# Moving the V loads of an attention and FFN kernel from SyncE's queue to GpSimd's

## The chip, the cores and the metric

The kernel runs on one core of a Trainium2 chip. The metric is the device time of one execution in microseconds (us). A run is called slow when it is over 1.5% above the fastest of the same kernel. "Faster", "same" and "slower" are drawn at 2%.

## The reference

Attention is computed inside chunks of 64 tokens; its output, laid out as tokens by 512, goes through two matrices with a squared ReLU between them.

```python
batch, n_heads, seq, head_dim = (8, 8, 576, 64)          # 4608 tokens of 512
n_tokens, d_model, d_ff = (4608, 512, 2048)
...
scores = scale * np.matmul(q_c, k_c.transpose(0, 1, 2, 4, 3))   # chunks of 64
attn = softmax(scores)                                          # cut
out = np.matmul(attn, v_c)
...
h = np.maximum(x @ w_in, 0.0)
return (h * h @ w_out).astype(np.float32)
```

## The kernel before

The 4608 tokens are 18 groups of 256; two groups make a block, and there are nine blocks, 0 to 8. While TensorE does the two FFN matrix products of block j, the attention of block j+1 (`nxt`) is threaded in between, and q, k and V of block j+2 (`far`) are loaded. Nearly all loads are issued from SyncE (`nc.sync`), nearly all stores of results from ScalarE.

```python
def v_pieces(g):                      # four or five loads for one group
    for t, p, m, b, s in runs(g):
        yield lambda ...: nc.sync.dma_start(
            out=v_even[g % NV][p:p + m, t, :, 0:D],
            in_=v[b, 0::2, s:s + m, :].rearrange("h s d -> s h d"))
    ...                               # the same for the odd heads, into v_odd

def cast_qk(g):                       # GpSimd: float32 to bfloat16
    qkb = att_pool.tile([128, 2, 2 * H * D], BF16, name="qkb", bufs=2)
    for which in range(2):
        nc.gpsimd.tensor_copy(out=qkb[:, which], in_=...)

def transpose_qk_dma(g):              # one DMA transposes q and k of a group
    qkT = att_pool.tile([128, 2, 2, n_hp, 128], BF16, name="qkT", bufs=4)
    nc.sync.dma_start_transpose(out=qkT..., in_=qkb...)
```

`scores` reads qkT with 32 small matmuls, `values` reads v_even and v_odd, and `transpose_x` brings the attention output x into the layout of the FFN, from block 3 on with two more DMA transposes a group from SyncE. In the second FFN product every 16 matmuls end in a copy and a store, both on ScalarE:

```python
nc.scalar.copy(out=o_sb, in_=o_ps)
nc.scalar.dma_start(out=out[t0:t0 + 128, :], in_=o_sb)
```

A plan lays these pieces into slots; a slot is four FFN matmuls. In each slot at most one load is issued.

```python
else:                                             # blocks 2 to 8
    loads, go_slots = pieces(far), range(32)      # q and k of both groups, then V
    d = {2: 5, 3: 2}.get(j, 0)
    for i, g in enumerate(nxt):
        for slot, f in ((4, SC), (8, AV), (11, XT)):
            at(slot + d if f is SC else slot + d + 3 * i, f, g)
    for i, g in enumerate(far):
        at(14 + 2 * i, C, g)                      # casts
        at(19 + 3 * i, TD, g)                     # DMA transposes of q and k
```

The softmax here doesn't subtract the row's maximum and nothing guards it: scores larger than these inputs give would overflow.

## Time and profile before

| | before |
|---|---|
| median of 3 runs | 302.27 us (299.15 to 306.41, the last of which counts as slow) |
| profiled span | 302.7 us |
| TensorE busy | 280.5 us, 93% |
| GpSimd busy | 49.4 us, 16% |
| DMA transposes of q and k, issue to landing, median | 4.9 us |

TensorE is nearly always busy, so what counts is when it isn't. The prediction reads the page, the stretches, the waits and SyncE's queue. Two more readings matter for what follows. The first is the view of the source line of the q and k transposes (columns of its first line: duration of the issuing instruction in ns as minimum, median and maximum, then first and last start in us):

```profile
L224 SPq DMA_TRANSPOSE qkT<-qkb x14: 1655/2552/3704, 69.1 to 233.3; - x14
...
DMA to landing us min/median/max: 4.0/4.9/6.5
```

No transpose needs more than 6.5 us. The second is the DMA view from 69 to 76 us, while the first pair of them is under way (a queue's packets, MB, and the time of its packets as a share of the 16 engines' time, which can pass 100%):

```profile
q1 hardware_dynamic: 5224, 1.31, 105.5%
```

All that moves here goes through one queue, q1: 1.31 MB at 209 GB/s, and the pair, issued from 69.10 on, has landed at 76.21.

### The profile page before, as it was taken

To read this page: it belongs to the slowest core of one execution; us is meant where nothing else is said; L and a number is where in the kernel's file an instruction comes from. 1 tells how busy PE (TensorE), PEld (TensorE's weight loads), DVE (VectorE), ACT (ScalarE), POOL (GpSimd) and SP (SyncE) were. 2 spreads that over 40 slices of the span, in tenths; PEclk is the share of its full clock that TensorE was granted. 3 is DMA by queue.
4 is the path that set the end of the run, shared out by engine and by line. 5 is a ranking of instruction groups with operands and counts; after the bars stand their busy time and mean duration, and the time that the engine had idled before them with its cause. 6 is when DMAs were issued, how large, how long until landed. Compare 5 with 4: busy or idle time off the path is not lost.

```text
span 302.7 us, 6379 instructions
## 1 busy us (share of the span) xinstructions
PE 280.5 (93%) x2564; PEld 141.3 (47%) x2598; DVE 113.0 (37%) x247; ACT 130.0 (43%) x225; POOL 49.4 (16%) x68
## 2 busy tenths in 40 slices
PE   2889979898899799899999997999999999999995
PEld 2654435784454444444444443444444444444442
DVE  1348613692234350353037203740482038104400
ACT  1536305674217621762176215731662186217511
POOL 2047820140130040023003201400230000000000
PEclk9999999999799999999999999999999999999999
DMA  7999999999999899999899899869997704211011
GB/s 207 243 347 365 342 264 246 237 206 212 217 213 211 194 191 205 224 215 193 195 250 211 148 229 269 171 104 254 267 183 157 182 37 37 69 69 38 0 69 69
DMA packets 158765, 57.04 MB, mean 188 GB/s; under 512 B 139664, under 2 KB 152208, under 8 KB 158736
## 3 DMA queue, kind: packets, MB, share of 16 engines
q1 hardware_dynamic: 153024, 46.81, 73.2%
q10 hardware_dynamic: 5712, 9.83, 10.4%
q8 instruction: 20, 0.33, 0.5%
q14 instruction: 9, 0.07, 0.1%
HBM read 36.70 MB, written 9.44 MB: 152 GB/s over the span
## 4 chain that ended last, share of the span: by engine, by line
PE 67%; DMA 18%; SPq 10%; issue 2%; POOL 1%; ACT 1%; DVE 0%; ACTq 0%
PE ps_ffn L319 31%; PE ps_ffn L335 27%; DMA qkT<-qkb 6%; DMA k_sb<-in_k_dram 6%; SPq L224 4%; DMA w_st<-in_moe_w_in_dram 4%; SPq L282 3%; PE ps_att L259 2%; PE ps_ffn L364 2%; DMA w_st<-in_moe_w_out_dram 2%; PE ps_att L238 2%; SPq L117 1%; PE ps_ffn L164 1%; SPq L124 1%; POOL w_in_bf L139 1%
## 5 line engine op out<-in xcount | busy, mean ns | idle before, releaser
L319 PE MATMUL ps_ffn<-xT,w_in_bf 128*128 128x512 bf16 (+1 forms) x620 | 128.6, 357 | 3.1 <-ACT rl L325 1.6
L326 DVE TENSOR_TENSOR gT<-rl 128x512 bf16<-128x512 bf16 (+1 forms) x160 | 75.5, 489 | 133.9 <-ACT rl L325 131.4
L335 PE MATMUL ps_ffn<-w_out_bf,gT 128*128 128x512 bf16 x500 | 113.0, 382 | 0.8 <-issue 0.3
L325 ACT ACTIVATE rl<-ps_ffn 128x512 bf16<-128x512 f32 (+1 forms) x160 | 86.2, 560 | 42.5 <-PE ps_ffn L319 31.0
L319 PEld LDWEIGHTS <-w_in_bf 128*128 128x128 bf16 x640 | 60.8, 98 | 60.9 <-issue 2.1
L335 PEld LDWEIGHTS <-gT 128*128 128x128 bf16 x512 | 49.9, 98 | 59.7 <-issue 1.3
L352 ACT COPY o_sb<-ps_ffn 128x512 f32<-128x512 f32 x31 | 18.2, 586 | 92.9 <-PE ps_ffn L335 79.7
L217 POOL CAST qkb<-q_sb 128x1024 bf16<-128x1024 f32 x14 | 14.7, 1048 | 146.9 <-DMA q_sb<-in_q_dram 126.6
L269 DVE TENSOR_TENSOR x<-ps_att,rec 128x512 bf16<-128x512 f32 x36 | 24.9, 691 | 1.2
L245 ACT ACTIVATE e<-ps_att 128x1024 bf16<-128x1024 f32 x18 | 18.2, 1037 | 5.5 <-PE ps_att L238 5.5
L217 POOL CAST qkb<-k_sb 128x1024 bf16<-128x1024 f32 x14 | 16.0, 1144 | 6.5 <-DMA k_sb<-in_k_dram 6.4
L364 PE MATMUL ps_ffn<-w_out_bf,gT 128*128 128x512 bf16 x62 | 14.4, 379 | 0.2 <-issue 0.2
L238 PE MATMUL ps_att<-qkT 64*64 64x64 bf16 x576 | 8.1, 198 | 6.0 <-DMA qkT<-qkb 4.6
L266 DVE RECIPROCAL rec<-ps_att 128x8 f32<-128x8 f32 x36 | 7.1, 199 | 15.4 <-PE ps_att L259 15.4
L139 POOL CAST w_in_bf<-w_st 128x1024 bf16<-128x1024 f32 (+1 forms) x9 | 8.8, 980 | 19.1 <-DMA w_st<-in_moe_w_in_dram 19.1
L238 PEld LDWEIGHTS <-qkT 64*64 64x64 bf16 x576 | 6.2, 110 | 10.8 <-DMA qkT<-qkb 6.1
L259 PEld LDWEIGHTS <-e 64*64 64x64 bf16 x576 | 6.8, 110 | 8.5 <-DVE x L269 3.0
L259 PE MATMUL ps_att<-vo_sb,e 64*64 64x65 bf16 x288 | 9.2, 199 | 0.8 <-DMA vo_sb<-in_v_dram 0.8
L364 PEld LDWEIGHTS <-gT 128*128 128x128 bf16 x64 | 6.0, 98 | 7.2 <-issue 0.3
L147 POOL CAST w_out_bf<-w_st 128x1024 bf16<-128x1024 f32 x8 | 8.7, 1091 | 2.7 <-DMA w_st<-in_moe_w_out_dram 2.6
L259 PE MATMUL ps_att<-ve_sb,e 64*64 64x65 bf16 x288 | 9.2, 199 | 0.0
L173 ACT COPY qkT<-ps_att 128x512 bf16<-128x512 bf16 x4 | 2.1, 589 | 13.9 <-DVE qkT L173 11.8
(31 smaller groups left out, 46.0 us busy)
## 6 DMA issues: line engine op xcount, KB each, us to landing
out_dram<-o_sb ACTq DMA_DIRECT2D x35, 256.0 KB, 3.3
q_sb<-in_q_dram SPq DMA_DIRECT2D x25, 256.0 KB, 4.8
k_sb<-in_k_dram SPq DMA_DIRECT2D x25, 256.0 KB, 5.3
ve_sb<-in_v_dram SPq DMA_DIRECT2D x32, 128.0 KB, 3.9
vo_sb<-in_v_dram SPq DMA_DIRECT2D x32, 128.0 KB, 3.9
w_st<-in_moe_w_out_dram SPq DMA_DIRECT2D x8, 512.0 KB, 5.7
w_st<-in_moe_w_in_dram SPq DMA_DIRECT2D x7, 512.0 KB, 7.3
q_sb<-in_q_dram SPq DMA_DIRECT2D x3, 512.0 KB, 6.6
```

Source lines behind the costliest of these rows:

```text
L217: nc.gpsimd.tensor_copy(out=qkb[:, which], in_=qk[g][which].rearrange("p t h d -> p (t h d)"))
L224: nc.sync.dma_start_transpose(out=qkT.rearrange("c w t h q -> c (w t h) q"), in_=qkb.rearrange("p w c -> p (w c)"))
L238: nc.tensor.matmul(out=ps[64 * c:64 * c + 64, o0:o0 + 64], lhsT=qkT[64 * a:64 * a + 64, 1, t, hp, cols], rhs=qkT[64 * a:64 * a + 64, 0, t, ...
L245: nc.scalar.activation(out=e.rearrange("p a h t q -> p (a h t q)"), in_=ps, func=AF.Exp, scale=scale)
L259: nc.tensor.matmul(out=ps[64 * p:64 * p + 64, a, hp * (D + 1):(hp + 1) * (D + 1)], lhsT=e[64 * c:64 * c + 64, a, hp, t, :], rhs=vb[64 * c: ...
L269: nc.vector.tensor_tensor(out=x.rearrange("p h a d -> p a h d"), in0=o[:, :, :, 0:D], in1=rec.to_broadcast([128, 2, n_hp, D]), op=ALU.mult)
L319: nc.tensor.matmul(out=h[:, 0:n], lhsT=w_in_bf[:, dt, ft * 128:(ft + 1) * 128], rhs=xT[:, dt, c:c + n], start=(dt == 0), stop=(dt == n_dt ...
L325: nc.scalar.activation(out=rl[:, 0:n], in_=h[:, 0:n], func=AF.Relu)
L326: nc.vector.tensor_tensor(out=gT[:, ft, c:c + n], in0=rl[:, 0:n], in1=rl[:, 0:n], op=ALU.mult)
L335: nc.tensor.matmul(out=o_ps, lhsT=gT[:, ft, tt * 128:(tt + 1) * 128], rhs=w_out_bf[:, ft, :], start=(ft == 0), stop=(ft == n_ft - 1))
L352: nc.scalar.copy(out=o_sb, in_=o_ps)
L364: nc.tensor.matmul(out=o_ps[tt], lhsT=gT[:, ft, tt * 128:(tt + 1) * 128], rhs=w_out_bf[:, ft, :], start=(ft == 0), stop=(ft == n_ft - 1))
```

## The change

The intent is to take the V loads out of SyncE's queue from block 1 on, so that the DMA transposes, which the scores wait for, needn't stand behind them. V is issued from GpSimd, whose engine is mostly idle, in every second slot of the first half of a block (in block 1 in the last 14 slots); and from block 3 on scores, values and x transposes come one or two slots later.

```diff
-    def v_pieces(g):
+    def v_pieces(g, eng=nc.sync):
...
-            yield lambda t=t, p=p, m=m, b=b, s=s: nc.sync.dma_start(
+            yield lambda t=t, p=p, m=m, b=b, s=s: eng.dma_start(
...
         elif j == 1:
-            go_slots = [*range(17), *range(34, 48)]
-            loads = itertools.chain(pieces(nxt), pieces(far))
+            go_slots, v_slots = [*range(17), *range(34, 48)], range(34, 48)
+            loads = itertools.chain(pieces(nxt), *map(qk_pieces, far))
...
         else:
-            loads, go_slots = pieces(far), range(32)
-            d = {2: 5, 3: 2}.get(j, 0)
-            if j == 2:
-                go_slots = [*range(10), *range(18, 32)]
+            go_slots, v_slots = range(16), range(0, 18, 2)
+            loads = itertools.chain(*map(qk_pieces, far))
+            d = {2: 5, 3: 3}.get(j, 2)
...
+        v_loads = itertools.chain(*(v_pieces(g, nc.gpsimd) for g in far if j))
...
-                if slot in go_slots:
-                    for f in loads:
-                        f()
-                        break
+                for queue, slots in ((loads, go_slots), (v_loads, v_slots)):
+                    if slot in slots:
+                        for f in queue:
+                            f()
+                            break
```

A slot only fixes the order in which the program hands instructions to the engines. It makes GpSimd wait for nothing.

More of the change, by code (lines that the diff above doesn't have):

```diff
@@ L123, in v_pieces @@
             for b, s, m in segments(lo, hi - lo):
-                yield lambda n=n, p=p, m=m, b=b, s=s: nc.sync.dma_start(
+                yield lambda n=n, p=p, m=m, b=b, s=s: eng.dma_start(
                     out=v_odd[n % NO][p:p + m, :, 0:D],
@@ L423 @@
         if j == 0:
-            loads, go_slots = iter(()), []
+            loads, go_slots, v_slots = iter(()), [], []
             for slot, f in ((24, T), (27, SC), (29, AV), (31, XT)):
@@ L461 @@
         go(loads)
+        go(v_loads)
         if j == 1:
```

## The prediction

> **What bounds the kernel now.** I read the busy table and the 40 slices first, then a table of busy time by stretch with one stretch for each of the nine blocks of 512 tokens, then the waits of TensorE, then the chain that ended last, and last the SyncE queue in order of time. The page:
>
> ```profile
> PE 280.5 (93%) x2564; PEld 141.3 (47%) x2598; DVE 113.0 (37%) x247; ACT 130.0 (43%) x225; POOL 49.4 (16%) x68
> ...
> PE   2889979898899799899999997999999999999995
> ...
> DMA  7999999999999899999899899869997704211011
> ```
>
> TensorE is busy nearly everywhere, and the 16 DMA engines are full for the first 25 slices or so. GpSimd has room: 16%. So TensorE is the bound, and only its gaps can be won. The stretches, cut where a block's first L319 matmul starts (columns: stretch, length, busy time of each engine, granted clock, DMA share, GB/s):
>
> ```profile
> 53.10:89.60 36.50, 33.55 (x410) 22.22 (x410) 18.51 (x49) 16.60 (x40) 8.44 (x8) 0.95 1.07 222
> 89.60:120.65 31.05, 29.34 (x253) 13.56 (x257) 10.69 (x24) 13.80 (x22) 4.36 (x4) 1.00 0.98 195
> 120.65:151.15 30.50, 29.34 (x253) 13.62 (x257) 10.10 (x24) 13.76 (x22) 4.50 (x4) 1.00 1.04 206
> 151.15:181.30 30.15, 29.34 (x254) 13.65 (x257) 10.27 (x24) 13.70 (x22) 4.11 (x4) 1.00 0.98 208
> 181.30:212.60 31.30, 29.52 (x254) 13.65 (x257) 11.69 (x24) 12.98 (x22) 4.58 (x4) 1.00 0.93 199
> 212.60:242.00 29.40, 29.19 (x254) 13.60 (x257) 12.01 (x24) 12.98 (x22) 4.43 (x4) 1.00 0.92 199
> ```
>
> The last row is block 6, which has no gap: 29.40 us is what such a block costs. Blocks 2, 3, 4 and 5 do the same work in 31.05, 30.50, 30.15 and 31.30, so they lose 1.65 + 1.10 + 0.75 + 1.90 = 5.4 us. Block 1 (36.50) has more attention work and a clock of 0.95; I count only its wait as reachable. The waits of TensorE over blocks 1 to 5 name the gaps:
>
> ```profile
> PE ps_att L238 <- DMA qkT<-qkb: 4.6, 4, 1.7
> PE ps_ffn L319 <- ACT rl L325: 1.6, 1, 1.6
> ```
>
> Four times the score matmuls wait for the DMA transpose of q and k: 1.67 us in block 1 (at 76 us), 1.39, 0.95 and 0.60 in blocks 2, 3 and 4. Once, at 186 us, TensorE waits for ScalarE, which had stood in its queue before a store; the chain leads from that store to a k load (4.07 us). Before the late transposes the chain runs through SyncE's queue. Block 3 in order of time there:
>
> ```profile
> 135.91 2.88 SPq L117 DMA_DIRECT2D ve_sb<-in_v_dram  x2
> 138.84 1.05 SPq L124 DMA_DIRECT2D vo_sb<-in_v_dram  x2
> 140.00 2.54 SPq L282 DMA_TRANSPOSE xT<-x  x2
> 142.59 1.93 SPq L117 DMA_DIRECT2D ve_sb<-in_v_dram  x3
> 144.62 2.55 SPq L282 DMA_TRANSPOSE xT<-x  x2
> 147.22 1.12 SPq L124 DMA_DIRECT2D vo_sb<-in_v_dram  x2
> 148.45 6.15 SPq L224 DMA_TRANSPOSE qkT<-qkb  x2
> ```
>
> There is no idle time of note here. x of block 4 was ready at about 138.5 us and the casts of q and k ended at 141.3, but the transposes of q and k leave from 148.45 on, because V loads and x transposes stand before them. The second lands at about 156.5; its scores stood ready at 156.0.
>
> **What the Trainium skill says.** "DMA: Bandwidth & Descriptors", Issuing engines are not separate DMA queues: whichever engine issues, the same 16 DMA engines carry the transfer, and only the issuer's sequencer time is saved. The trace agrees that sequencer time is the matter here (SyncE's queue is on the chain, GpSimd's nowhere), and it warns that bytes are not made fewer. Same page, SWDGE vs HWDGE vs iDMA: DMAs issued from GpSimd get their descriptors from software on the GpSimd cores, while SyncE's are made by hardware. The kernel before issues none from GpSimd, so no row gives the price of one with 512 runs of 256 bytes; this is the largest unknown. "SBUF — State Buffer", Who interferes with whom: a VectorE instruction with both inputs in SBUF contends with a GpSimd instruction that reads SBUF. The trace agrees: the squaring at L326 takes 0.42 us alone and 0.86 at 135.94, beside a cast that itself took 1.31 instead of 1.04. The section says that one which only writes SBUF is spared, so descriptor writing may cost VectorE nothing; no run here shows that yet.
>
> **The change part by part.**
>
> Removed from SyncE: counting the pieces that the code makes, groups 6 to 17 have 53 V loads of the 80, eight or nine in a block. In block 3 they held the queue for 2.88 + 1.05 + 1.93 + 1.12 = 7.0 us, of 27.0 in all (q and k loads 8.8, V 7.0, x transposes 5.1, q/k transposes 6.15) in a block of 30.5. Without them the queue needs 20 us a block and waits at the x transposes for x instead. The q/k transposes can then leave as soon as x and the casts are done, about 141.5 instead of 148.45: some 7 us earlier, with a gap of at most 1.67 us to close.
>
> Moved in the plan: from block 4 on scores, values and x transposes come two slots later (block 3: one). A slot is four matmuls, 0.86 us in the trace, so the transposes get 1.7 us more (0.9 in block 3). That alone covers the 0.60 us of block 4. It costs TensorE nothing: the same matmuls in another order, and x is needed only at the next block's start, 14 slots on.
>
> Added to GpSimd: nine V DMAs a block beside four casts (4.4 us). GpSimd may use 29.4 - 4.4 = 25.0 us before it is the bound itself, so 25.0 / 9 = 2.8 us per V load is the break-even. I choose 1 to 2.5 us as likely, a guess that no row supports; 2 us would make GpSimd 22.4 us busy in 29.4. GpSimd is not held to the slots: it starts the V loads as soon as it has done the casts of the block before. So in block 1, after the cast at 66.3, V loads of block 3 run beside the q/k transposes of 69 to 76 and before the casts at 82 to 89. At 2 us they end at 67.5 + 18 = 85.5, the casts at about 90, and the transposes leave at about 90 instead of 94.25.
>
> DMA: bytes are the same. A block moves 3.15 MB of q, k, v, 1.05 of output and 1.57 of transposes, 5.8 MB; in 29.4 us that is 196 GB/s, against 195 to 208 measured at a share near 1. So it just fits, with no room for much more.
>
> The sum: of the waits for qkT I take 1.4 + 1.0 + 0.6 from blocks 2 to 4 and 0.8 of 1.67 from block 1 (V traffic now shares the engines with those very transposes); the stall in block 5 comes from the order of stores and loads, so I take half of it, 1.0. That is 4.8 us. I give back 0.3 for VectorE held up by GpSimd and V arriving late once. 302.27 - 4.5 = 297.8 us.
>
> **Rivals.** First, GpSimd becomes the bound. If one V load takes 3.3 us, a block needs 9 x 3.3 + 4.4 = 34 us of GpSimd, 4.7 more than TensorE. The casts sit behind the V loads in the same queue, so the wait moves from SyncE to GpSimd and grows: over the six V-loading blocks, less the slack at the start, 10 to 20 us more, 310 to 320 us. For it: many small runs and software; against it: GpSimd is idle for 84% of the span, and it starts a block's V loads early. Second, the DMA engines are the true limit and SyncE's durations are only back-pressure. For it: a share of 0.98 to 1.07 through blocks 1 to 4. Then qkT still comes late by what it was, only the later slots help, and the time is 300 to 302. Against it: block 6 ran without a gap at a share of 0.92 and 199 GB/s. Third, more is won than I count: the granted clock of block 1 fell to 0.95 after the 1.67 us gap, and without the gap some 1.5 us more come back; with all of block 5's loss as well the time is about 294.
>
> **Range and chances.** The middle is 298. The third rival sets the lower end at 291, with a little for the spread of the runs before (299.15 to 306.41). The first sets the upper end, but I hold it half likely at most to bite partly: 309. Over 2% faster means under 296.2, which needs nearly everything: 0.33. Within 2%: 0.49. Slower than 308.3 needs GpSimd as the bound: 0.18.
>
> **What would show it.** Right: no row of TensorE waiting for qkT after block 2, blocks 3 to 5 at 29.4 to 29.8 us, SyncE waiting at L282 for x for several us in each block, the L224 issues some 5 to 7 us earlier in their block, the V loads on GpSimd's queue at 1 to 2.5 us each. Wrong: V loads of 3 us and more, GpSimd's casts no longer waiting for q and k loads but following V loads without a gap, score matmuls waiting longer for qkT, or value matmuls waiting for ve_sb and vo_sb; or L326 well above its mean of 524 ns, with ScalarE waiting for it. If instead the share of DMA stays at 1.0 and qkT lands later after its issue than the 4.9 us of now, the second rival was right.

## The result

| | before | after |
|---|---|---|
| median (lowest to highest), runs | 301.83 us (299.15 to 306.41), 4 | 321.82 us (318.07 to 328.85), 4 |
| profiled span | 302.7 us | 320.8 us |
| mean granted clock | 0.994 | 0.96 |
| q and k transposes, issue to landing, median | 4.9 us | 7.3 us |
| x transposes, the same | 3.1 us | 5.4 us |

One run of each four is slow (306.41 and 328.85). The changed kernel is slower: the ratio of fast runs is 1.065, with a 95% interval of 1.050 to 1.080. All ratios here are the mean time of one kernel's fast runs over that of the other's of the same rounds, so they are not quite the ratio of the medians quoted.

The page of the changed kernel (busy tenths of TensorE in 40 slices of 8 us, and the granted clock in tenths):

```profile
PE   2889978992599999179999999999899999999995
...
PEclk9999999997599999759999999999999999999999
```

Two holes stand out, in slices 10 and 11 and in slices 17 and 18, and the granted clock falls with each of them. The stretches of the two blocks, columns as in the prediction's table:

```profile
52.90:97.00 44.10, 33.74 (x408) 22.43 (x410) 18.83 (x49) 16.30 (x40) 16.50 (x20) 0.88 1.13 213
126.40:168.40 42.00, 32.89 (x253) 14.29 (x257) 10.73 (x24) 13.12 (x22) 10.79 (x13) 0.84 1.01 176
```

Block 1 takes 44.1 us where it took 36.5, block 3 takes 42.0 where it took 30.5. Cut where each block's first matmul begins (block 8 is counted up to TensorE's last matmul), the blocks compare so:

| block | 0 | 1 | 2 | 3 | 4 | 5 | 6 | 7 | 8 |
|---|---|---|---|---|---|---|---|---|---|
| before, us | 33.5 | 36.5 | 31.1 | 30.5 | 30.2 | 31.2 | 29.4 | 29.4 | 27.8 |
| after, us | 33.3 | 44.1 | 29.4 | 42.0 | 30.2 | 29.4 | 32.0 | 29.4 | 27.8 |

Blocks 1, 3 and 6 lose 7.7 + 11.5 + 2.6 us, blocks 2 and 5 win 1.7 + 1.9 (from unrounded times). GpSimd's own work is not the reason. Its rows on the page, and the queue of its transfers:

```profile
L117 POOL DMA_DIRECT2D ve_sb<-in_v_dram x27 | 19.5, 727 | 0.0
...
q0 software_dynamic: 2368, 6.23, 11.8%
```

One V load costs GpSimd 0.73 us, and it is busy for 27% of the span. It holds up others little: its casts of q take 1063 ns in the mean (before: 1048), VectorE's squarings 502 (before: 489). What changed are the transposes, in the view of their source line:

```profile
L224 SPq DMA_TRANSPOSE qkT<-qkb x14: 1665/3828/10948, 68.8 to 251.3; - x14
...
DMA to landing us min/median/max: 5.1/7.3/16.4
```

The minimum has gone from 4.0 to 5.1 us, the maximum from 6.5 to 16.4. The waits of all engines (total us, times, longest) say who paid:

```profile
ACT o_sb L352 <- DMA qkT<-qkb: 15.5, 2, 12.1
...
PE ps_att L238 <- DMA qkT<-qkb: 8.9, 2, 5.9
PE ps_ffn L319 <- ACT o_sb L352: 7.4, 1, 7.4
```

**Block 1.** The score matmuls wait twice for qkT, 5.90 and 3.00 us, at 74 to 84 us. The queues there, in order of time (start, duration, engine):

```profile
68.81 11.21 SPq L224 DMA_TRANSPOSE qkT<-qkb  x2
...
67.18 2.12 POOL L117 DMA_DIRECT2D ve_sb<-in_v_dram  x3
...
72.25 1.49 POOL L124 DMA_DIRECT2D vo_sb<-in_v_dram  x2
```

The pair of transposes is issued at the same time as before (69.10), but its issue takes 11.21 us and not 4.78, and from first issue to last landing it needs 14.67 us and not 7.11. Nine V loads of block 3 are issued from 67.18 to 73.74, because GpSimd had done a cast at 67.2 and had nothing to wait for. The DMA view from 69 to 83 us:

```profile
q1 hardware_dynamic: 5348, 1.34, 70.7%
q0 software_dynamic: 399, 1.05, 37.4%
```

SyncE's queue moves about the bytes that it moved from 69 to 76 us before, and 1.05 MB of V come in between, so it takes twice as long. The rate of both together is 191 GB/s, where it was 209. At 191 GB/s the V loads alone are 5.5 us (an estimate from these figures), of a delay of 7.6 us: most of it is bandwidth shared. In the worst two microseconds, 76 to 78:

```profile
q0 software_dynamic: 159, 0.41, 92.8%
q1 hardware_dynamic: 39, 0.01, 2.4%
```

There the engines carry V for block 3, which begins at 126.4 us, and hardly anything of the queue with the transposes that TensorE stands waiting for. The packets also differ: in the transfer kernel further down six V loads of 0.79 MB in all are 288 packets from GpSimd, its data packets of 4096 bytes, and 3168 from ScalarE, some 250 bytes each.

**Block 3.** Nothing waits for qkT directly. The first pair of transposes for block 4 is issued at 118.87, again while V loads (116.8 to 122.5) are on their way, and takes 15.84 us to issue; to its last landing it needs 17.85 us (before: 10.82). ScalarE and TensorE in order of time:

```profile
123.10 0.58 ACT L352 COPY o_sb<-ps_ffn 128x512 f32<-128x512 f32 x1 [2.87 <-PE ps_ffn L335]
135.34 0.40 ACTq L353 DMA_DIRECT2D out_dram<-o_sb  x1
135.83 0.58 ACT L352 COPY o_sb<-ps_ffn 128x512 f32<-128x512 f32 x1 [12.14 <-DMA qkT<-qkb]
...
136.47 1.86 PE L319 MATMUL ps_ffn<-xT,w_in_bf 128*128 128x512 bf16 x4 [7.36 <-ACT o_sb L352]
```

The copy is done at 123.7, yet its store is issued only at 135.34; the first transpose of the pair has landed at 135.26. The store needs no qkT. But in the program as built there are eight completion semaphores for the DMAs of SyncE and ScalarE, used in turn, and an instruction that starts a DMA waits first for the DMA that last used its semaphore. The trace shows that this store's turn fell behind the late transpose: the transpose issued at 118.87 raises semaphore 108, ScalarE waits for 108 until 135.28, and its store, issued then, raises 108 itself. The experiment with the stores on another queue tests it. ScalarE stood in its queue, nobody emptied the PSUM banks, and TensorE stopped for 7.36 us. The prediction had seen the same kind of stall at 186 us of the kernel before.

**The clock.** The idle part of block 3 (length less busy time) grew from 1.2 to 9.1 us, and its busy time from 29.3 to 32.9 for the same matmuls. A stretch of that block after the gap:

```profile
138.00:142.00 4.00, 2.46 (x7) 0.73 (x6) 1.70 (x4) 2.29 (x5) 0.56 (x1) 0.50 1.18 291
```

The granted clock is 0.50 there, 0.60 in the next 4 us, then 1.00. The Trainium skill has this: "TensorE: Matmul & The Clock Gate", Part 1, says that the array falls to half rate after an idle window of about 3.4 us and comes back after about as long a busy one. The trace agrees that the clock falls after idle time (0.50 after the gap of 7.36 us, and from 76.9 to 87.2 us in block 1), and in block 3 it cost 3.6 us. It doesn't confirm the length: in the kernel before the clock fell as well, where TensorE's longest gap was 1.67 us and it was busy for 1.58 of 3.41 us:

```profile
73.76:77.17 3.41, 1.58 (x68) 0.97 (x68) 0.00 (x0) 1.60 (x3) 0.00 (x0) 1.00 1.12 250
77.17:80.58 3.41, 3.41 (x40) 1.26 (x39) 0.37 (x2) 0.61 (x1) 0.00 (x0) 0.50 1.31 229
```

### The profile page after: what moved, and what is told of

It reads as the page before. It is cut to its first block, busy times and chain, and to the rows that moved or that the text cites.

```text
span 320.8 us, 6409 instructions
## 1 busy us (share of the span) xinstructions
PE 284.4 (89%) x2564; PEld 142.3 (44%) x2598; DVE 114.8 (36%) x247; ACT 128.4 (40%) x225; POOL 87.0 (27%) x121
## 4 chain that ended last, share of the span: by engine, by line
PE 51%; DMA 17%; SPq 16%; DVE 6%; issue 4%; POOL 3%; ACT 3%; ACTq 0%; POOLq 0%
PE ps_ffn L319 24%; PE ps_ffn L335 21%; SPq L224 12%; DMA k_sb<-in_k_dram 6%; DMA w_st<-in_moe_w_in_dram 4%; DMA q_sb<-in_q_dram 3%; DVE gT L326 3%; SPq L110 2%; DMA vo_sb<-in_v_dram 2%; ACT rl L325 2%; PE ps_ffn L364 2%; DMA w_st<-in_moe_w_out_dram 2%; DVE x L269 2%; SPq L282 1%; PE ps_att L238 1%
## 5 line engine op out<-in xcount | busy, mean ns | idle before, releaser
L319 PE MATMUL ps_ffn<-xT,w_in_bf 128*128 128x512 bf16 (+1 forms) x624 | 132.7, 364 | 11.7 <-ACT o_sb L352 7.4
L326 DVE TENSOR_TENSOR gT<-rl 128x512 bf16<-128x512 bf16 (+1 forms) x160 | 77.3, 502 | 142.7 <-ACT rl L325 139.6
L325 ACT ACTIVATE rl<-ps_ffn 128x512 bf16<-128x512 f32 (+1 forms) x160 | 85.0, 559 | 45.8 <-PE ps_ffn L319 29.3
L319 PEld LDWEIGHTS <-w_in_bf 128*128 128x128 bf16 x640 | 61.6, 99 | 72.9 <-issue 16.1
L335 PEld LDWEIGHTS <-gT 128*128 128x128 bf16 x512 | 50.1, 99 | 59.9 <-issue 1.6
L217 POOL CAST qkb<-q_sb 128x1024 bf16<-128x1024 f32 x14 | 14.9, 1063 | 130.2 <-DMA q_sb<-in_q_dram 109.5
L117 POOL DMA_DIRECT2D ve_sb<-in_v_dram x27 | 19.5, 727 | 0.0
L124 POOL DMA_DIRECT2D vo_sb<-in_v_dram x26 | 18.8, 727 | 0.0
L364 PE MATMUL ps_ffn<-w_out_bf,gT 128*128 128x512 bf16 x62 | 14.4, 379 | 0.2 <-issue 0.2
```

Source lines behind the costliest of these rows:

```text
L117: yield lambda t=t, p=p, m=m, b=b, s=s: eng.dma_start(out=v_even[g % NV][p:p + m, t, :, 0:D], in_=v[b, 0::2, s:s + m, :].rearrange("h s d ...
L124: yield lambda n=n, p=p, m=m, b=b, s=s: eng.dma_start(out=v_odd[n % NO][p:p + m, :, 0:D], in_=v[b, 1::2, s:s + m, :].rearrange("h s d -> s ...
L217: nc.gpsimd.tensor_copy(out=qkb[:, which], in_=qk[g][which].rearrange("p t h d -> p (t h d)"))
L319: nc.tensor.matmul(out=h[:, 0:n], lhsT=w_in_bf[:, dt, ft * 128:(ft + 1) * 128], rhs=xT[:, dt, c:c + n], start=(dt == 0), stop=(dt == n_dt ...
L325: nc.scalar.activation(out=rl[:, 0:n], in_=h[:, 0:n], func=AF.Relu)
L326: nc.vector.tensor_tensor(out=gT[:, ft, c:c + n], in0=rl[:, 0:n], in1=rl[:, 0:n], op=ALU.mult)
```

## The experiments

The theory, called A: V's traffic meets the q and k transposes at the DMA engines, which SyncE's one queue had kept apart, and they land late. In its form A1 any traffic beside them does this, whoever issues it; in its form A2 it is GpSimd's own kind of transfer (its queue, its large packets). The rivals: the new plan of slots does it; ScalarE's stalled store is a cause and not a consequence; GpSimd's added work slows casts or VectorE. Kernels of a group ran on one chip and share the runs of the kernel before. All but those said to be wrong gave correct results.

The first four ran together (before: median 299.75 us, 298.56 to 301.95, 7 runs).

### The new plan, with V still on SyncE

```diff
# against the changed kernel
-        v_loads = itertools.chain(*(v_pieces(g, nc.gpsimd) for g in far if j))
+        v_loads = itertools.chain(*(v_pieces(g, nc.sync) for g in far if j))
```

> The changed plan (q and k loads first, V slots, scores two slots later) but V issued by SyncE, so no transfer from GpSimd's queue. Theory A (transfers from GpSimd's queue, in flight beside the DMA transposes of q and k, slow those transposes): the transposes go back to about 5 us from issue to landing and the time to 297-303 us. Rival B (the new plan is at fault: the transposes, the loads and the stores now stand in a bad order): the time stays at 316-325 us.

Measured: 303.44 us (302.75 to 303.88), ratio 1.012 (1.007 to 1.017). The transposes in the view of their line, and TensorE's only wait for them:

```profile
DMA to landing us min/median/max: 3.9/5.2/5.7
...
PE ps_att L238 <- DMA qkT<-qkb: 3.6, 1, 3.6
```

With the same plan and the same loads, only issued elsewhere, nothing lands later than 5.7 us. So the plan is not what costs 6.5%. It costs a little by itself, and wins nothing: block 1 ends 2.7 us earlier than in the kernel before (86.9 us, 89.6), and block 2 gives it back in a wait of 3.6 us for qkT; block 3 begins at 122.1 us (before: 120.7).

### The old plan, with V on GpSimd

```diff
# against the kernel before
     def v_pieces(g):
+        eng = nc.gpsimd if g >= 6 else nc.sync
...
-            yield lambda t=t, p=p, m=m, b=b, s=s: nc.sync.dma_start(
+            yield lambda t=t, p=p, m=m, b=b, s=s: eng.dma_start(
```

> The kernel before with nothing changed but the queue of the V loads of groups 6 to 17: GpSimd. Theory A: the q/k transposes take 7 us and more from issue to landing (median; up to 16) and the time is 312-325 us. Rival B (the plan): 298-304 us, transposes near 5 us.

Measured: 315.92 us (310.87 to 328.27), ratio 1.043 (1.033 to 1.053) from the two fast runs of four: slower. The transposes land after 6.8 us in the median and 14.0 at most, and the score matmuls wait 10.2 us for them. Block 1 takes 45.4 us. The engine of issue alone brings most of the loss.

### V held back behind the transposes

GpSimd reads one column of the next block's two qkT tiles before the first V load of a block, so it can't start V while they are in flight.

```diff
# against the changed kernel, shortened
+        def hold(f):
+            for g in nxt:
+                nc.gpsimd.tensor_copy(
+                    out=gate[:, 0:1], in_=qkTs[g][:, 1, 1, n_hp - 1, 127:128])
+            f()
+        # called for the first V load of a block only
```

> The changed kernel, but GpSimd reads one column of the transposed q/k tiles of the block before it issues the first V load of a block, so that no V load of that block is in flight beside those transposes. Theory A: transposes back to about 5 us, no gap of TensorE over 2 us in blocks 1 and 3, 295-301 us. Rival C (DMAs with software-made descriptors are bad by themselves: they burden GpSimd, VectorE or the DMA engines wherever they are): little better than the changed kernel, 312-325 us.

Measured: 306.28 us (305.89 to 306.44), ratio 1.021 (1.016 to 1.027), class "unclear". That lies between what the theory (295 to 301) and its rival C (312 to 325) had forecast, so both missed. Two thirds of the loss are gone, with V still on GpSimd and 12 instructions more on it, so GpSimd's work as such isn't the cause. A part of what is left fits the theory. SyncE's queue:

```profile
86.61 10.50 SPq L227 DMA_TRANSPOSE qkT<-qkb  x2
```

The V loads of block 3, held back to 78 to 84.6 us, now run into the next pair of transposes, at 86.61; the first of it needs 10.0 us to land. The rest isn't explained by V from GpSimd: blocks 1 and 3 take 38.1 and 34.7 us (before: 36.5, 30.5), though their pairs met none of it. The pair of block 1 takes 6.59 us (after: 11.21), that of block 3 4.52 us (after: 15.84).

### V on ScalarE's queue

```diff
# against the changed kernel
-        v_loads = itertools.chain(*(v_pieces(g, nc.gpsimd) for g in far if j))
+        v_loads = itertools.chain(*(v_pieces(g, nc.scalar) for g in far if j))
```

> The changed kernel with V issued by ScalarE's hardware queue instead of GpSimd's: a second queue, but hardware descriptors. If any second queue with loads slows the transposes (A1), they take 7 us and more again. If it is the software-made descriptors with their packets of 2.6 KB (A2), the transposes take about 5 us. The total says less, since ScalarE's own instructions stand behind these issues (0.34 us each, and their waits): 300-320 us under A2, over 315 under A1.

Measured: 303.40 us (301.46 to 304.64), ratio 1.012 (1.005 to 1.018); transposes 4.6 us in the median, 8.0 at most. A second queue for V does little harm here. But this doesn't tell A1 from A2: ScalarE has FFN work in every slot, so its V loads stay in their slots (123 to 137 us, 153 to 166) and from block 3 on don't meet the transposes (113.8, 140.9, 169.5). The first two pairs did meet some: three V loads at 67.81, where the pair took 8.7 us from first issue to last landing, and six at 88.17, where it took 9.9 us and its first transpose 8.0. But a pair at that place takes as long without it (10.1 us with V on SyncE, 8.6 with no V at all). So V in another queue is harmless when it comes at another time; the few meetings decide nothing.

The next four ran on another chip (before: median 300.96 us, 298.6 to 304.08, 27 runs).

### The transfers by themselves

A kernel of nothing but transfers: two transposes of the size of q and k, V loads, stores, in phases that wait for each other. Its output is wrong, which doesn't matter for the time.

```python
for phase in (lambda: tr(), lambda: vl(P, 6), lambda: vl(A, 6),
              lambda: (tr(), vl(P, 6)), lambda: (tr(), vl(A, 6)), ...):
    gate()      # all of the phase before has landed
    phase()     # P: issued from GpSimd, A: from ScalarE
```

> Wrong result on purpose: no attention, no matmuls, only the transfers, in twelve phases, each begun when all of the last one has landed, the twelve done twice. Two q/k transposes alone; six V loads (128 KB each) from GpSimd alone, from ScalarE alone; the transposes beside each; beside two V loads from GpSimd; beside eight of a quarter of the size; beside four stores of 256 KB from ScalarE; the stores alone; four q loads alone, beside four V loads from GpSimd, and from ScalarE. Theory A2 (big packets of the software queue take turns with the small ones of the transposes): alone 5 to 6 us for the pair, beside six V loads from GpSimd 9 to 14, beside ScalarE's V loads of 256-byte packets at most 8; stores with 2 KB packets slow them as much for each byte as V from GpSimd does; plain q loads beside V from GpSimd suffer like the transposes. Rival D (something between a transpose and the software queue alone): plain q loads beside V from GpSimd take about the sum of both alone, while the transposes take clearly more than their sum; stores slow them little.

Measured, from the first issue to the last landing of the transposes, in two repeats:

| phase | us |
|---|---|
| transposes alone | 6.9, 6.8 |
| beside six V loads from GpSimd | 8.6, 9.3 |
| beside six V loads from ScalarE | 9.2, 10.0 |
| beside two V loads from GpSimd | 8.3, 8.4 |
| beside four stores from ScalarE | 8.0, 7.8 |
| four q loads alone (their own landing) | 6.6, 6.5 |
| four q loads beside four V loads from GpSimd | 8.6, 8.4 |

From GpSimd it was a weak test, since V came some 3.5 us behind the transposes. From ScalarE it came 0.5 us behind:

```profile
57.53 5.56 SPq L67 DMA_TRANSPOSE tt<-src  x2
...
58.03 5.30 ACTq L73 DMA_DIRECT2D vv<-in_v_dram  x6
```

So V from ScalarE, where it does meet the transposes, delays them by 2.3 and 3.2 us. A2 had forecast at most 8 us there, and missed. Plain q loads are delayed by V as well, so it isn't a matter of the transposes alone.

### The stores on SyncE

```diff
# against the changed kernel
-                    nc.scalar.dma_start(out=out[t0:t0 + 128, :], in_=o_sb)
+                    nc.sync.dma_start(out=out[t0:t0 + 128, :], in_=o_sb)
```

> The changed kernel with the output stores of blocks 1 to 8 issued by SyncE instead of ScalarE. Theory: the 7.4 us gap of TensorE in block 3 is ScalarE standing before a store that waits for the completion of a late transpose, with relu and copies behind it. Then that gap goes and the time falls by 6 to 11 us, to 308-315, while the waits for qkT in block 1 (8.9 us) stay. Rival: the gap is ScalarE waiting for something else in the DMA engines; the time stays within 3 us of the changed kernel.

Measured: one fast run of 310.23 us and three slow ones up to 321.22; no ratio is given, and the profiled run is a slow one, so only its shape is used. The fast run lies in the forecast range. The gap of block 3 is gone (29.4 us), as it must be if ScalarE's store was the link. But blocks 1 and 2 take 46.9 and 36.9 us, and the score matmuls now wait directly:

```profile
PE ps_att L238 <- DMA qkT<-qkb: 15.2, 3, 5.6
```

The stall of the store is a consequence. Take it away, and the late transposes are still late (five of seven pairs take 8.5 to 11.5 us) and stop TensorE elsewhere. The edit also puts the stores into SyncE's queue, so it changes what stands before the transposes as well.

### The kernel before with later scores

This asks whether the gain that the prediction hoped for was there at all, without any move of V.

```diff
# against the kernel before
-                for slot, f in (..., (36, SC), (38 + 2 * i, AV), (42 + 2 * i, XT)):
+                for slot, f in (..., (38, SC), (40 + 2 * i, AV), (43 + 2 * i, XT)):
...
-            d = {2: 5, 3: 2}.get(j, 0)
+            d = {2: 7, 3: 4}.get(j, 2)
```

> The kernel before with scores, values and x transposes two slots later in every block from block 1 on, V still on SyncE. If the waits for qkT that the prediction counted (4.6 us of TensorE) can be had by later slots alone: 2 to 4 us faster than before, 0.6 to 1.3 per cent. If the transfers set the pace of the early blocks, a gap closed in one block opens in another: within 0.4 per cent of before.

Measured: 301.73 us (300.24 to 304.83, 22 runs, one of them slow), ratio 1.004 (1.001 to 1.007). Block 1 shrinks from 36.5 to 33.7 us, block 2 grows from 31.1 to 33.7, and block 3 begins at 120.1 us, before at 120.7. A gap closed in block 1 opens again in block 2.

### Half of V on GpSimd

```diff
# against the changed kernel: the odd heads stay on SyncE
-                yield lambda n=n, p=p, m=m, b=b, s=s: eng.dma_start(
+                yield lambda n=n, p=p, m=m, b=b, s=s: nc.sync.dma_start(
```

> The changed kernel with only the V loads of even heads on GpSimd and those of odd heads on SyncE. If the harm grows with the bytes of the software queue in flight beside the transposes: about half of it, 308-314 us, pairs of transposes at 6 to 9 us of issue. If any transfer of that queue does the whole harm: 316 us and more. If it needs GpSimd's queue to be full: 300-305.

Measured: 313.22 us (310.56 to 318.73, one slow run), ratio 1.040 (1.032 to 1.049); the class on record is "unclear". Transposes 6.0 us in the median and 11.4 at most, and 6.8 us of waiting for qkT. Half of the loads bring more than half of the loss; block 1 alone takes 43.9 us.

The next two ran on a third chip (before: median 302.14 us, 299.31 to 303.83, 7 runs).

### The transfers by themselves, V first

The same kind of kernel, wrong, with two V loads issued ahead of the transposes and the rest beside them, as in the changed kernel. The transposes wait for a GpSimd instruction; time is taken from its end to the last landing.

```python
lambda: go_tr(),                                   # alone
lambda: (vl(P, 2), go_tr(), vl2(P, 2, 6)),         # 2 V loads, transposes, 4 V loads
lambda: (vl(P, 2), go_tr(), vl2(P, 2, 4), st(2)),  # and two stores
```

> Wrong result on purpose, transfers alone as in the first such run, but with V in flight before the transposes, as in the changed kernel (there they came after the transposes and cost only some 2 us). Phases, each twice: the two q/k transposes alone (7 us from the first issue to the last landing, as measured there); two V loads from GpSimd, the transposes, four more V loads; six V loads from ScalarE and the transposes 1 us later; six V loads from GpSimd, then the transposes; two V, transposes, two V and two stores of 256 KB from ScalarE; the same without the stores; the same with V from ScalarE; transposes and two, then four stores; eight V loads of a quarter of the size from GpSimd. If the transfers alone do it: 11 us and more for the transposes beside V from GpSimd, or at least beside V and stores together, and 9 or less beside V from ScalarE. If it needs the work of the other engines: at most 9 us in every phase.

| phase | us, two repeats |
|---|---|
| transposes alone | 6.9, 6.9 |
| 2 V loads from GpSimd, transposes, 4 V loads | 9.6, 9.7 |
| 6 V loads from ScalarE begun 4 us ahead, transposes | 6.9, 6.9 |
| 6 V loads from GpSimd begun 4.6 us ahead, transposes | 7.1, 7.3 |
| 2 V loads from GpSimd, transposes, 2 V loads | 8.2, 8.5 |
| the same with two stores | 10.6, 9.6 |
| the same with two stores, V from ScalarE | 8.4, 8.3 |
| transposes and two stores | 8.3, 8.3 |
| transposes and four stores | 10.2, 10.1 |

Six loads of which four come behind the transposes cost them 2.7 us, four stores 3.2, and six loads begun 4 us ahead next to nothing from either engine. Both forecasts, 11 us and more or at most 9, missed. With the six loads the first landing moved from 4.6 to 8.2 us.

### No V loads at all

```diff
# against the kernel before; wrong on purpose
     def v_pieces(g):
+        if g >= 6:
+            return
```

> Wrong result on purpose: the kernel before without the V loads of groups 6 to 17 (the value matmuls read the old tiles). It is the ceiling of anything that can be won by moving them. If the transfers set the pace of blocks 1 and 2: block 3 begins 4 to 8 us earlier than in the kernel before (120.7 us) and the time falls to 292-296. If the waits for qkT were only SyncE's order, as the prediction had it: 295-298, with block 3 about 3 us earlier.

Measured: 297.13 us (296.65 to 299.42), ratio 0.984 (0.978 to 0.990), class "unclear". This is the ceiling: even if V came for nothing, 1.6% is to be had. Its blocks 2 to 7 take 29.4 us each, and block 3 begins at 116.9 us, 3.8 us earlier than before. The outcome lies between the two forecasts (a transfer limit, 292 to 296 us; SyncE's order, 295 to 298), so it doesn't tell which of them holds up the first blocks.

### The transfers beside working engines

The transfer kernel with more V behind the transposes, and with VectorE squarings, matmuls or q loads beside them. Wrong; run on a fourth chip (before: one run, 303.50 us), at a granted clock of 0.675 in the mean.

```python
def mix():                # 2 V loads, transposes, 6 V loads
    vl(P, 2); go_tr(); vl2(P, 2, 8)
lambda: (mix(), st(2)), lambda: (dve(), mix(), st(2)), lambda: (pe(), mix(), st(2)),
lambda: (ql(), mix(), st(2)), ...
```

> Wrong result on purpose, transfers by themselves again, now with work of the other engines beside them. Ten phases, each twice: the two q/k transposes alone (6.9 us from release to the last landing, as measured); beside 36 squarings of VectorE (bf16, both inputs in SBUF, as L326); beside 72 matmuls of 512 columns; behind two of eight V loads from GpSimd (mix); mix with two stores of 256 KB; that with the squarings; with the matmuls; with both; with four q loads of 256 KB ahead of it in SyncE's queue; and four x transposes in place of the two. If the work of the other engines makes the transposes late in the changed kernel (up to 16 us): a phase with squarings or matmuls takes 3 us and more over the same phase without. If it is only traffic: mix with stores 11 to 13 us whatever the engines do, and with the q loads ahead 15 us and more.

Measured in two repeats, to the last landing of the transposes: alone 7.0 and 6.9 us; mix 10.5 and 10.8; mix and two stores 12.6 and 13.3; with squarings 13.2 and 12.8, with matmuls 13.4 and 14.4, with both 12.6 and 12.6; with four q loads ahead of the mix 15.2 and 14.1. The traffic does it, and the engines' other work adds at most 1.1 us in the same repeat. The last phase comes near block 3's pair (17.9 us from first issue to last landing) with transfers alone, though not all the way.

### The same overlap from three queues

Run on a fifth chip (before: one run, 303.02 us). It should have told A1 from A2: the same phase with V from GpSimd, ScalarE and SyncE. Its output is wrong, which doesn't matter for the time.

```python
lambda: (vl(P, 2), go_tr(), vl2(P, 2, 6)),           # GpSimd
lambda: (vl0(), vl(A, 2), go_tr(), vl2(A, 2, 6)),    # ScalarE
lambda: (vl0(), vl(S, 2), go_tr(), vl2(S, 2, 6)),    # SyncE
lambda: (vl0(), vl(S, 6), go_tr()),                  # SyncE, all ahead
```

> Wrong results on purpose: nothing but transfers, each phase three times, timed from a GpSimd memset to GpSimd's read after the last landing. One block's q and k transposes with V loads in the same order, 2 loads, the transposes, 4 loads, with only the queue of the V loads changed. In the run of the transfers by themselves this took 6.9 us without V and 9.6 to 9.7 us with V from GpSimd. A1 (it is the traffic, whoever issues it): from ScalarE's queue and from SyncE's the same phase takes within 0.5 us of GpSimd's, 9.1 to 10.1 us. A2 (it is GpSimd's own kind of transfer, with its packets of 4096 bytes): ScalarE's at most 8.3 us. Six loads alone: about the same from GpSimd and SyncE, 6 to 7 us, in both.

Measured from the release, the transposes took 9.2, 9.2 and 9.9 us with V from GpSimd, 6.9, 7.7 and 7.6 from ScalarE, 6.9 in all three with two loads ahead and four behind on SyncE, 7.0, 7.1 and 6.9 alone. By the text, that is A2. But the trace shows that the test failed in its construction:

```profile
128.78 1.49 POOL L74 DMA_DIRECT2D vv<-in_v_dram  x2
...
130.40 7.03 SPq L68 DMA_TRANSPOSE tt<-src  x2
...
143.50 0.94 ACTq L74 DMA_DIRECT2D vv<-in_v_dram  x2
...
147.15 4.54 SPq L68 DMA_TRANSPOSE tt<-src  x2
```

ScalarE had nothing to wait for and began V 3.65 us ahead of the transposes, GpSimd 1.6 us ahead. So the overlap isn't the same. Counted from the first V load to the last landing, which doesn't depend on that, the work takes 10.9, 10.8 and 11.5 us from GpSimd, 10.5, 11.3 and 11.2 from ScalarE, and 11.0, 11.0 and 10.8 from SyncE with all V ahead. The sum of V and transposes takes equally long whoever issues it. Which queue V takes decides who goes first: behind SyncE's transposes in one queue, V costs them nothing (6.9 us), while V in a queue of its own takes its share from them. Six V loads alone took 6.4 to 6.7 us from GpSimd and 5.5 to 5.7 us from SyncE.

## Why the prediction was wrong

**The bound and the gaps** were read rightly: TensorE is the bound and only its gaps count. The gaps of block 2 did close (31.1 to 29.4 us), and SyncE now waits for x, 49.8 us in nine waits, as foretold. The transposes left earlier in their block, as foretold too: 21.9 us after its start in block 2 (before: 27.7), 19.6 in block 4 (25.1), 18.5 in block 5 (23.5).

**GpSimd's cost.** The guess of 1 to 2.5 us per V load was too high; it is 0.73 us. That GpSimd is so quick made the meeting denser: nine loads left it within 6.6 us in block 1, where 18 had been foreseen; what a slower GpSimd would have cost was not tried. The first rival had the direction of the time right and the mechanism wrong: GpSimd never became the bound.

**The step that failed** is the charge for V beside the transposes. The prediction saw that in block 1 "V loads of block 3 run beside the q/k transposes of 69 to 76", and charged 0.87 us for it, by taking only 0.8 of the 1.67 us of block 1 as won. The term was mis-sized: block 1 lost 7.7 us, and block 3, where the same meeting happens at 117 to 135 us and nothing was charged, 11.5 us; block 6 lost 2.6 us, where the pair at 217 us took 10.31 us. Behind the mis-sizing stands the sentence "DMA: bytes are the same" with its conclusion "it just fits". The bytes fit over a block, but not in the 5 us in which a transpose has to land. The prediction took SyncE's order for a mere obstacle (V stands before the transposes). It was also a protection (V stands behind them), as the new plan with V on SyncE shows: 5.7 us at most.

**What made the loss larger than the delay** were two things that the sum lacked. A late transpose holds a completion semaphore whose next user is a store, so ScalarE stood for 12.1 us and TensorE for 7.36; the stores on SyncE removed that gap, and the transposes stayed late. And after such a gap the granted clock is 0.50 for some microseconds, which cost 3.6 us in block 3. The prediction used the clock only for the upside.

**The gain of 4.8 us** wasn't there either. It was read from one profiled run of 304.47 us and subtracted from the median of 302.27; fast runs of the unchanged kernel reach 298.6. Where V meets the transposes little or not at all (the new plan on SyncE, later scores, ScalarE's queue) the ratios are 1.012, 1.004 and 1.012. With V on SyncE or left as it was, a gap closed in block 1 opens again in block 2: block 3 begins at 122.1 us with the new plan on SyncE and at 120.1 with later scores, before at 120.7. This looks like the second rival, a limit set by the transfers, but it isn't settled: block 3 begins at 116.9 us without V, and at 118.9 with all of V on ScalarE's queue. The rival's sign, qkT landing later than 4.9 us, did come (7.3 us), but it speaks for V's queue: with the same plan and V on SyncE it is 5.2.

**What stays open.** First, how much of it is GpSimd's own. With transfers alone ScalarE's V, where it met the transposes, cost them 2.3 and 3.2 us, GpSimd's 1.8 to 3.0, and four stores 3.2; so A1 holds there, and GpSimd's queue or its large packets aren't needed for a delay of this size. In the whole kernel no version made ScalarE's V meet the transposes as densely as GpSimd's does, so whether the large packets make the delays of 14.7 and 17.9 us worse is not shown. Second, why the engines move so little when all meet in block 3. From 119 to 135 us the DMA view of the kernel before has first

```profile
q1 hardware_dynamic: 11760, 2.95, 101.9%
```

and that of the changed kernel

```profile
q1 hardware_dynamic: 3322, 0.83, 62.3%
q0 software_dynamic: 350, 0.91, 45.2%
```

A packet of q1 took 1.019 x 256 / 11760 = 22 ns of an engine before (16 engines by 16 us), and 0.623 x 256 / 3322 = 48 ns after. By themselves, with V from GpSimd beside them, they took 22 ns. The total rate fell from 219 to 125 GB/s. The transfer kernels come near the same delay with q loads and stores in the mix, so it needs no other engine, but what happens inside the DMA engines no run here shows.

No version beats the kernel before, and the ceiling of 1.6% says that there is little to look for in V.

## What to carry to other kernels

A queue's order is also a priority: before moving "unimportant" loads out of the way of urgent ones, look at what will then be in flight beside the urgent ones, in the few microseconds in which they must land, not at the bytes of a block. An engine with little to do runs ahead of any slot plan, so loads moved to it need a wait of their own to come at the right time. And charge a gap of several microseconds on TensorE with the clock that it costs afterwards, and a late DMA with everyone who shares its completion semaphore.

## What the Trainium skill lacked or had wrong

- "DMA: Bandwidth & Descriptors", Issuing engines are not separate DMA queues: it says that issuing from several engines only saves the time on the sequencer. The trace agrees that the same 16 engines carry everything, but the choice is not neutral: 53 loads moved to GpSimd made the kernel 4.3% slower with the old plan and 6.5% with the new one, and with the new one the q and k transposes went from 6.5 us at most to 16.4. The section lacks what follows from a queue's order for the choice of queue: with two V loads ahead of the transposes and four behind, those in SyncE's own queue cost them nothing (6.9 us), those in GpSimd's 2.1 to 3.0 us.
- The same page, Queues, rings and completion order, has each engine take turns between queues packet by packet. No run here confirms or refutes it: from 76 to 78 us the engines took 159 packets of GpSimd's queue and 39 of SyncE's, but no view shows which queue had packets ready, and SyncE was still issuing until 80.02. What it lacks is how far the packets of two engines can differ: for the same six V loads 288 from GpSimd and 3168 from ScalarE.
- The same page, SWDGE vs HWDGE vs iDMA, gives no price for a load from GpSimd with 512 runs of 256 bytes: 0.73 us of GpSimd each, and it doesn't grow when the engines are full.
- No page that I read has the cost of sharing completion semaphores in turn between unrelated DMAs: a store that needed nothing waited 11.6 us (123.7 to 135.34) for a transpose.
- "TensorE: Matmul & The Clock Gate", Part 1, doesn't say how much work a stretch may hold and still lower the clock: with 1.58 us of 3.41 busy, and no gap over 1.67 us, it was 0.50 in the next 3.41 us.
